# Residual rows loaded into the finished value columns of a weight tile, and the last two output blocks computed in column halves

## The chip, the cores and the metric

The kernel runs on one core of a Trainium2 chip. That core has five engines that run at the same time, each through its own list of instructions in order: TensorE for matrix products (PE in the profile, with its loads of the stationary operand listed apart as PEld), VectorE (DVE), ScalarE (ACT), GpSimd (POOL) and SyncE (SP). Data moves between the chip's main memory and the core's working memory (SBUF) by DMA. Here DMAs are started by SP, ACT and POOL, each with a queue of its own: q1 is SP's, q10 is ACT's and q0 is POOL's. Matrix products accumulate in PSUM, which has eight banks of 512 float32 columns per partition.

The metric is the device time of one execution in microseconds (us). Before the change it is 259.9 us, the median of three runs (259.37 to 260.32 us).

## The reference

The input `x` has 2048 tokens of width 512. It is normalised once. One branch is attention with 32 heads of width 16, in which a token sees itself and the 255 tokens before it. The other is a gated MLP whose gate mixes all tokens. The output is `x` plus both branches, so every block of output rows needs the same block of rows of `x` once more: these rows are called the residual here.

```python
def _A_ref(x, wqkv, wo):
    B, S, D = x.shape          # 1, 2048, 512
    H = 32; Dh = D // H; W = 256
    qkv = (lambda x, *d: x.transpose(*d))((x @ wqkv).reshape(B, S, 3, H, Dh), 2, 0, 3, 1, 4)
    q, k, v = (qkv[0], qkv[1], qkv[2])
    scores = jnp.einsum('bhqd,bhkd->bhqk', q, k) * Dh ** (-0.5)
    idx = jnp.arange(S)
    mask = (idx[:, None] - idx[None, :] >= 0) & (idx[:, None] - idx[None, :] < W)
    p = _softmax(jnp.where(mask[None, None], scores, -1000000000.0), axis=-1)
    o = jnp.einsum('bhqk,bhkd->bhqd', p, v)
    return (lambda x, *d: x.transpose(*d))(o, 0, 2, 1, 3).reshape(B, S, D) @ wo

def _B_ref(x, w_in, w_sp, b_sp, w_out):
    z = _gelu(jnp.einsum('bsd,df->bsf', x, w_in))       # 2048 x 1376
    z1 = z[..., :688]
    z2 = _layernorm(z[..., 688:], axis=-1)
    g = jnp.einsum('ts,bsf->btf', w_sp, z2) + b_sp[None, :, None]
    return jnp.einsum('bsf,fd->bsd', z1 * g, w_out)

xn = _layernorm(A_x, axis=-1)
return A_x + _A_ref(xn, A_wqkv, A_wo) + _B_ref(xn, B_w_in, B_w_sp, B_b_sp, B_w_out)
```

## The kernel before

Tokens are cut into 16 blocks of 128 rows (`n` = 0 to 15). Heads are cut into four groups of eight (`G` = 0 to 3). The order of all work is written out by hand in three strings, `STAGE1`, `STAGE2` and `STAGE3`: each token such as `O,15,k,0,1` names a step by a letter and gives its arguments. The table `ops` maps letters to functions, and `run` calls them in the order of the string. Each engine then works through its own share of the steps in that order, and waits only where its data or its buffer is not ready.

Stage 1 normalises `x`, computes the gated activations and starts the projections. Stage 2 runs the attention: for each group, `S` computes scores (L429, PE), `X` takes their exponentials (L443, ACT), `M` masks them (L452 and L460, DVE), `V` multiplies by the values (L510, PE), and `N` normalises the result and transposes it into `oT` (L518 to L531, DVE). Between these, PE does projections (`Q`, `K`, `P`: L339 and L394), the token mixing (`H`, L551) and at the end the output products. `F` and `G` spread projected queries and keys by DMAs on the POOL queue (L366 and L387; for the last head groups `F,3,3` and `G,3,3` are the last of them). `u` transposes a block of the MLP's result by a DMA on the SP queue (L564).

An output block `n` is made by these steps:

- `r,n` (`load_xres`, L574): POOL issues a DMA that loads the block's 128 x 512 residual rows into a tile `x_ch`. The tile comes from the pool `cpool`, which gives it two buffers. The load of one block therefore waits until the add of the block two loads earlier has read its buffer.
- `O,n,bank,c0,c1` (`out_u`, L580): PE multiplies by the MLP's output weights, six products of 128 x 512 in all; `R,n,bank,c0,c1` (`out_o`, L586) adds the attention's output product, four more, one for each head group, into the same PSUM bank.
- `o,n,bank` (`keep_out`, L594): DVE adds PSUM and the residual into a tile `out_sb`, also with two buffers.
- `v,n` (`store_out`, L601): a DMA writes 128 KB to the output. It is issued on POOL's queue for block 0 and on SP's for the others.

Banks `w` and `v` serve the blocks up to 11 in turn. In stage 3 the four banks that the scores used are free, and blocks 13, 12, 15 and 14 use the banks `i`, `j`, `k` and `l`. The adds come in the order 0 1 3 2 5 4 6 7 8 9 11 10 13 12 15 14.

The weights of all three projections stay in one tile, `wqkv`, of 128 partitions x 4 chunks x 1536 columns. Columns 0 to 1023 of each chunk are read by `Q` and `K`, columns 1024 to 1535 by `P` alone, whose last step stands early in stage 2.

Of the kernel before, what the change touches and what calls it, by code (L numbers as in the profile page):

```python
# [22 lines left out]
NDC = D // P  # L23
NG = 4
# [4 lines left out]
NFC = UPAD // P  # L29
# [113 lines left out]
H,13,1,v,6,7 K,3,2,w,2,4 H,13,1,v,7,13 k,3,2,w,D M,13 S,2,9,0 G,3,2 H,13,1,v,13,16 X,2,9,0  # L143
H,14,0,w,0,6 h,13,1,v M,14 u,8 V,22 M,15 r,1 S,3,0,0 H,14,0,w,6,7 Q,3,2,v,0,1 X,3,0,0 N,21,0
H,14,0,w,7,8 Q,3,2,v,1,2 H,14,0,w,8,10 Q,3,2,v,2,3 H,14,0,w,10,16 u,9 h,14,0,w S,3,0,1 V,23
X,3,0,1 N,21,1 H,14,1,w,0,3 N,22,0 Q,3,2,v,3,4 H,14,1,w,3,8 q,3,2,v,D S,3,1,0 H,14,1,w,8,16
X,3,1,0 M,0 F,3,2 u,10 M,1 H,15,0,v,0,7 h,14,1,w N,22,1 S,3,1,1 V,24 X,3,1,1 H,15,0,v,7,16 u,11
M,2 S,3,2,0 H,15,1,w,0,6 X,3,2,0 h,15,0,v Q,3,3,v,0,4 H,15,1,w,6,8 q,3,3,v,D u,12 S,3,2,1
H,15,1,w,8,9 M,3 F,3,3 K,3,3,v,0,2 X,3,2,1 H,15,1,w,9,13 N,23,0 K,3,3,v,2,3 H,15,1,w,13,15
K,3,3,v,3,4 N,23,1 H,15,1,w,15,16 k,3,3,v,A S,3,3,0 V,25 h,15,1,w X,3,3,0 N,24,0 O,1,v,0,1  # L150
O,0,w,0,6 N,24,1 S,3,3,1 M,4 R,0,w,0,1 X,3,3,1 O,1,v,1,2 R,0,w,1,2 O,1,v,2,4 R,0,w,2,3 O,1,v,4,6
R,0,w,3,4 R,1,v,0,1 o,0,w S,3,4,0 R,1,v,1,4 X,3,4,0 M,5 v,0 O,3,w,0,3 o,1,v V,26 v,1 r,3 N,25,0
r,2 S,3,4,1 O,2,v,0,2 X,3,4,1 O,3,w,3,6 M,6 R,3,w,0,2 N,25,1 O,2,v,2,3 R,3,w,2,3 O,2,v,3,4 M,7
S,3,5,0 O,2,v,4,6 X,3,5,0 R,3,w,3,4 R,2,v,0,4 o,3,w v,3 r,5 V,27 o,2,v S,3,5,1 N,26,0 v,2 r,4
O,5,w,0,5 u,13 X,3,5,1 G,3,3 O,4,v,0,1 O,5,w,5,6 R,5,w,0,2 O,4,v,1,2 M,8 S,3,6,0 O,4,v,2,6
X,3,6,0 N,26,1 R,4,v,0,2 M,9 R,5,w,2,4 R,4,v,2,4 o,5,w S,3,6,1 o,4,v V,28 r,7 X,3,6,1 v,4 r,6
N,27,0 O,6,w,0,1 O,7,v,0,1 v,5 O,6,w,1,3 O,7,v,1,3 O,6,w,3,4 M,10 S,3,7,0 O,7,v,3,5 N,27,1
X,3,7,0 O,6,w,4,6 R,6,w,0,2 O,7,v,5,6 R,6,w,2,4 R,7,v,0,1 o,6,w S,3,7,1 R,7,v,1,3 X,3,7,1 v,6
r,8 O,8,w,0,1 u,14 R,7,v,3,4 O,8,w,1,6 o,7,v M,11 r,9 v,7 O,9,v,0,1 S,3,8,0 M,12 V,29 X,3,8,0
N,28,0 O,9,v,1,3 R,8,w,0,1 O,9,v,3,5 N,28,1 R,8,w,1,3 S,3,8,1 O,9,v,5,6 X,3,8,1 R,8,w,3,4  # L160
R,9,v,0,4 o,8,w r,10 O,11,w,0,6 o,9,v M,13 v,9 r,11 v,8 O,10,v,0,1 M,14 S,3,9,0 u,15 V,30
X,3,9,0
"""

STAGE3 = """
N,29,0 R,11,w,0,1 O,10,v,1,2 R,11,w,1,2 O,10,v,2,5 N,29,1 R,11,w,2,3 O,13,i,0,1 O,10,v,5,6 M,15
# [9 lines left out]
def kernel(  # L176
# [31 lines left out]
    oT = pers.tile([P, NG, S_TOK], BF, name="oT")  # L208
# [14 lines left out]
    banks = {"v": w0[:], "w": w1[:]}  # L223
# [345 lines left out]
    x_tiles = {}  # L569
    out_tiles = {}  # L570

    def load_xres(n):
        x_ch = cpool.tile([P, D], BF, name="x_ch")
        nc.gpsimd.dma_start(out=x_ch[:], in_=x2[n * P : (n + 1) * P, :])  # L574
# [16 lines left out]
    def keep_out(n, bank):  # L591
        out_sb = cpool.tile([P, D], BF, name="out_sb")
        out_tiles[n] = out_sb
        nc.vector.tensor_tensor(  # L594
            out=out_sb[:], in0=banks[bank], in1=x_tiles.pop(n)[:], op=ALU.add
        )

    def store_out(n):

        eng = nc.gpsimd if n == 0 else nc.sync  # L600
        eng.dma_start(out=out2[n * P : (n + 1) * P, :], in_=out_tiles.pop(n)[:])  # L601

    def set_o():
# [80 lines left out]
    for r0 in (0, 64):  # L684
        nc.gpsimd.affine_select(
            out=mask[r0 : r0 + 64, 0, :], in_=mask[r0 : r0 + 64, 0, :], pattern=[[-1, 64]],
# [3 lines left out]
            out=mask[r0 : r0 + 64, 1, :], in_=mask[r0 : r0 + 64, 1, :], pattern=[[1, 64]],  # L690
# [54 lines left out]
```

## Time and profile before

| what | value |
|---|---|
| median of three runs | 259.9 us |
| the profiled execution, its own time | 258.91 us |
| its span, from its first to its last instruction | 257.1 us |
| VectorE, ScalarE, GpSimd busy | 186.0, 181.0, 90.9 us |
| residual loads, 16 on POOL's queue, 128 KB each | 3.8 us from issue to landing (median) |
| output stores, 15 on SP's queue, 128 KB each | 1.9 us from issue to landing (median) |
| the output store on POOL's queue | 2.1 us |

A row of the timeline gives the start and the length of a group of alike instructions on one engine, in us from the start of the span. Then come the engine, the line of the program, the operation, the tile written and the tile read with their shapes, and the count. In brackets stands how long the engine was idle before it, and what ended that idle time. The ends of matmuls are modelled by the profiler, and since matmuls are pipelined, the distance between the starts of two neighbours is shorter than the length of one. Some matmul records can be missing. "DMA to landing" is the time from the issue of a DMA to the arrival of its last byte. A row of the view by form gives a group's total busy time and the mean length of one instruction in nanoseconds.

### The profile page before, as it was taken

To read this page: it belongs to the slowest core of one execution; us is meant where nothing else is said; L and a number is where in the kernel's file an instruction comes from. 1 tells how busy PE (TensorE), PEld (TensorE's weight loads), DVE (VectorE), ACT (ScalarE), POOL (GpSimd) and SP (SyncE) were. 2 spreads that over 40 slices of the span, in tenths; PEclk is the share of its full clock that TensorE was granted. 3 is DMA by queue.
4 is the path that set the end of the run, shared out by engine and by line. 5 is a ranking of instruction groups with operands and counts; after the bars stand their busy time and mean duration, and the time that the engine had idled before them with its cause. 6 is when DMAs were issued, how large, how long until landed. Compare 5 with 4: busy or idle time off the path is not lost. (4 is left out here: it accounts for less than half of the span.)

```text
span 257.1 us, 9010 instructions
## 1 busy us (share of the span) xinstructions
PE 248.5 (97%) x3880; PEld 137.1 (53%) x3916; DVE 186.0 (72%) x410; ACT 181.0 (70%) x142; POOL 90.9 (35%) x170
## 2 busy tenths in 40 slices
PE   7999999999999999999999999999999999999994
PEld 6565555433456555555555655655656544444541
DVE  4887877888797686778684776857877577667763
ACT  3686476899978687777868777776777786767400
POOL 7524110430015176017197055505545142511120
PEclk9999999999999999999999999999999999999999
DMA  7995743289404897749669476997755532764433
GB/s 237 362 247 98 118 82 83 61 134 234 96 3 95 102 145 144 129 98 170 116 122 165 105 101 118 123 161 128 156 123 96 94 74 84 112 128 116 115 102 102
DMA packets 69847, 32.65 MB, mean 127 GB/s; under 512 B 60800, under 2 KB 66912, under 8 KB 69808
## 3 DMA queue, kind: packets, MB, share of 16 engines
q1 hardware_dynamic: 64288, 21.19, 44.9%
q0 software_dynamic: 4576, 9.71, 17.6%
q10 hardware_dynamic: 944, 1.19, 1.3%
q8 instruction: 30, 0.49, 0.9%
q14 instruction: 9, 0.07, 0.1%
HBM read 8.41 MB, written 2.10 MB: 41 GB/s over the span
## 5 line engine op out<-in xcount | busy, mean ns | idle before, releaser
L443 ACT ACTIVATE E<-sS 128x2048 bf16<-128x2048 f32 x76 | 142.6, 1877 | 41.9 <-PE sS L429 40.8
L551 PE MATMUL w<-z,wspT 128*128 128x344 bf16 x512 | 92.6, 310 | 0.7 <-DVE z1u L558 0.2
L551 PEld LDWEIGHTS <-wspT 128*128 128x128 bf16 x512 | 46.9, 98 | 31.5 <-issue 5.9
L387 POOL DMA_DIRECT2D kbd<-kz x48 | 29.5, 622 | 59.8 <-DVE kz L379 57.7
L366 POOL DMA_DIRECT2D q<-qs x54 | 28.0, 527 | 30.5 <-DVE qs L355 23.1
L452 DVE TENSOR_TENSOR E<-E,mask 128x1024 bf16<-128x1024 bf16 x52 | 34.7, 676 | 4.3 <-ACT E L443 4.3
L339 PE MATMUL w<-xnT,wqkv 128*128 128x512 bf16 x106 | 35.7, 380 | 0.7 <-issue 0.3
L429 PE MATMUL sS<-q,kbd 32*128 32x320 bf16 (+4 forms) x816 | 30.4, 244 | 0.5 <-ACT E L443 0.2
L558 DVE SCALAR_TENSOR_TENSOR z1u<-w,b_all,z1u 128x344 bf16<-128x344 f32 x32 | 18.2, 568 | 16.3 <-PE w L551 16.2
L518 DVE STREAM_TRANSPOSE a<-oP 128x512 f32<-128x512 f32 x32 | 22.7, 709 | 4.7 <-PE oP L510 4.6
L309 PEld LDWEIGHTS <-xnT 128*128 128x128 bf16 x208 | 18.3, 98 | 12.4
L510 PE MATMUL oP<-E,v_all 64*17 64x256 bf16 (+3 forms) x1920 | 24.7, 230 | 0.0
L510 PEld LDWEIGHTS <-v_all 64*17 64x17 bf16 x1920 | 20.2, 85 | 8.4 <-issue 8.1
L429 PEld LDWEIGHTS <-kbd 32*128 32x128 bf16 x816 | 12.3, 92 | 22.3 <-issue 19.9
L580 PE MATMUL w<-w_out_sb,z1u 128*128 128x512 bf16 x67 | 19.1, 380 | 0.7 <-issue 0.3
L574 POOL DMA_DIRECT2D x_ch<-in_A_x_dram x16 | 8.8, 552 | 27.8 <-DVE out_sb L594 23.5
L339 PEld LDWEIGHTS <-wqkv 128*128 128x128 bf16 x128 | 12.1, 98 | 9.7 <-issue 1.2
L327 DVE BATCH_NORM_STATS2 st<-z 128x6 f32<-128x344 bf16 x32 | 14.4, 493 | 2.7 <-ACT z L322 2.7
L394 PE MATMUL w<-wqkv,xnT 128*128 128x512 bf16 x63 | 16.2, 379 | 0.0
L531 DVE STREAM_TRANSPOSE oT<-b 128x256 bf16<-128x256 bf16 x32 | 14.3, 445 | 1.1
L379 DVE CAST kz<-w 128x256 bf16<-128x256 f32 x26 | 9.8, 418 | 6.8 <-PE w L339 5.3
L580 PEld LDWEIGHTS <-z1u 128*128 128x128 bf16 x96 | 8.6, 97 | 10.2 <-issue 1.2
(90 smaller groups left out, 248.4 us busy)
## 6 DMA issues: line engine op xcount, KB each, us to landing
kbd<-kz POOLq DMA_DIRECT2D x48, 64.0 KB, 3.4
q<-qs POOLq DMA_DIRECT2D x36, 64.0 KB, 3.1
x_ch<-in_A_x_dram POOLq DMA_DIRECT2D x16, 128.0 KB, 3.8
out_dram<-out_sb SPq DMA_DIRECT2D x15, 128.0 KB, 1.9
wqkv<-in_A_wqkv_dram SPq DMA_DIRECT2D x1, 1536.0 KB, 12.0
xs<-in_A_x_dram SPq DMA_DIRECT2D x2, 512.0 KB, 7.2
kbd<-kz SPq DMA_DIRECT2D x16, 64.0 KB, 2.2
q<-qs SPq DMA_DIRECT2D x14, 64.0 KB, 2.0
```

Source lines behind the costliest of these rows:

```text
L309: nc.tensor.matmul(zp[:, lo:hi], lhsT=xcT[:, n, c, :] if n < NCEN else xnT[:, c, n * P : (n + 1) * P], rhs=w_in_sb[:, c, f0 + lo : f0 + hi ...
L339: nc.tensor.matmul(banks[bank], lhsT=wqkv[:, c, col : col + P], rhs=xnT[:, c, tok : tok + 512], start=(c == 0), stop=(c == NDC - 1),)
L366: eng.dma_start(out=q2[h : P : 2, e, c : c + w], in_=t[64 * e : 64 * e + 64, src0 + at : src0 + at + w],)
L387: eng.dma_start(out=kbd[h : P : 2, slot : slot + 4, e, :], in_=t[64 * e : 64 * e + 64, h, :].rearrange("p (k m) -> p k m", k=4),)
L429: nc.tensor.matmul(s_bank(s)[:, off + o : off + o + w], lhsT=kbd[32 * s : 32 * s + 32, slot, ee, :], rhs=q2[32 * s : 32 * s + 32, ee, c : ...
L443: nc.scalar.activation(out=dst, in_=src, func=ACT.Exp, scale=SM_SCALE)
L452: nc.vector.tensor_tensor(out=reg, in0=reg, in1=mask[:].rearrange("p a m -> p (a m)").unsqueeze(1).to_broadcast([P, 8, 128]), op=ALU.mult,)
L510: nc.tensor.matmul(skip_group_check=True, **args)
L518: nc.vector.transpose(out=a32[:].rearrange("p e c r -> p (e c r)"), in_=oP[i % 2][:])
L551: nc.tensor.matmul(banks[bank][:, 0:FQ], lhsT=w[:, c, :], rhs=z2[:, c, half * FQ : (half + 1) * FQ], start=(c == 0), stop=(c == NB - 1),)
L558: nc.vector.scalar_tensor_tensor(out=u, in0=banks[bank][:, 0:FQ], scalar=b_all[:, n : n + 1], in1=u, op0=ALU.add, op1=ALU.mult,)
L580: nc.tensor.matmul(banks[bank], lhsT=uT[:, c, :], rhs=w_out_sb[:, c, :], start=(c == 0), stop=False)
```

## The change

Three things change.

1. A residual load no longer writes a tile of its own. `load_xres(n)` writes into `wqkv[:, n % 4, 1024:1536]`, so there are four places in turn. The loads `r,2` to `r,15` stand earlier in the written order: `r,2` and `r,3` among the scores of the last head group, and each later one right behind the add that frees its place. The pool `cpool` gets four buffers instead of two, for `out_sb` alone.
2. The stores of blocks 1 and 2 go on POOL's queue, as that of block 0 did.
3. Blocks 15 and 14 are computed in two column halves of 256, each half in a PSUM bank of its own (`k` and `w`, `l` and `v`). Twenty products of 512 columns become forty of 256. Each half has its own add, and its own store of 64 KB: the left halves on SP's queue, the right halves on ACT's.

```diff
-X,3,0,1 N,21,1 H,14,1,w,0,3 N,22,0 Q,3,2,v,3,4 H,14,1,w,3,8 q,3,2,v,D S,3,1,0 H,14,1,w,8,16
+X,3,0,1 N,21,1 H,14,1,w,0,3 N,22,0 Q,3,2,v,3,4 H,14,1,w,3,8 q,3,2,v,D S,3,1,0 r,2 H,14,1,w,8,16
 X,3,1,0 M,0 F,3,2 u,10 M,1 H,15,0,v,0,7 h,14,1,w N,22,1 S,3,1,1 V,24 X,3,1,1 H,15,0,v,7,16 u,11
-M,2 S,3,2,0 H,15,1,w,0,6 X,3,2,0 h,15,0,v Q,3,3,v,0,4 H,15,1,w,6,8 q,3,3,v,D u,12 S,3,2,1
+M,2 S,3,2,0 r,3 H,15,1,w,0,6 X,3,2,0 h,15,0,v Q,3,3,v,0,4 H,15,1,w,6,8 q,3,3,v,D u,12 S,3,2,1
 H,15,1,w,8,9 M,3 F,3,3 K,3,3,v,0,2 X,3,2,1 H,15,1,w,9,13 N,23,0 K,3,3,v,2,3 H,15,1,w,13,15
 K,3,3,v,3,4 N,23,1 H,15,1,w,15,16 k,3,3,v,A S,3,3,0 V,25 h,15,1,w X,3,3,0 N,24,0 O,1,v,0,1
 O,0,w,0,6 N,24,1 S,3,3,1 M,4 R,0,w,0,1 X,3,3,1 O,1,v,1,2 R,0,w,1,2 O,1,v,2,4 R,0,w,2,3 O,1,v,4,6
-R,0,w,3,4 R,1,v,0,1 o,0,w S,3,4,0 R,1,v,1,4 X,3,4,0 M,5 v,0 O,3,w,0,3 o,1,v V,26 v,1 r,3 N,25,0
-r,2 S,3,4,1 O,2,v,0,2 X,3,4,1 O,3,w,3,6 M,6 R,3,w,0,2 N,25,1 O,2,v,2,3 R,3,w,2,3 O,2,v,3,4 M,7
-S,3,5,0 O,2,v,4,6 X,3,5,0 R,3,w,3,4 R,2,v,0,4 o,3,w v,3 r,5 V,27 o,2,v S,3,5,1 N,26,0 v,2 r,4
-O,5,w,0,5 u,13 X,3,5,1 G,3,3 O,4,v,0,1 O,5,w,5,6 R,5,w,0,2 O,4,v,1,2 M,8 S,3,6,0 O,4,v,2,6
-X,3,6,0 N,26,1 R,4,v,0,2 M,9 R,5,w,2,4 R,4,v,2,4 o,5,w S,3,6,1 o,4,v V,28 r,7 X,3,6,1 v,4 r,6
+R,0,w,3,4 R,1,v,0,1 o,0,w r,4 S,3,4,0 R,1,v,1,4 X,3,4,0 M,5 v,0 O,3,w,0,3 o,1,v r,5 V,26 v,1
+N,25,0 S,3,4,1 O,2,v,0,2 X,3,4,1 O,3,w,3,6 M,6 R,3,w,0,2 N,25,1 O,2,v,2,3 R,3,w,2,3 O,2,v,3,4
+M,7 S,3,5,0 O,2,v,4,6 X,3,5,0 R,3,w,3,4 R,2,v,0,4 o,3,w r,7 v,3 V,27 o,2,v r,6 S,3,5,1 N,26,0
+v,2 O,5,w,0,5 u,13 X,3,5,1 G,3,3 O,4,v,0,1 O,5,w,5,6 R,5,w,0,2 O,4,v,1,2 M,8 S,3,6,0 O,4,v,2,6
+X,3,6,0 N,26,1 R,4,v,0,2 M,9 R,5,w,2,4 R,4,v,2,4 o,5,w r,9 S,3,6,1 o,4,v r,8 V,28 X,3,6,1 v,4
 N,27,0 O,6,w,0,1 O,7,v,0,1 v,5 O,6,w,1,3 O,7,v,1,3 O,6,w,3,4 M,10 S,3,7,0 O,7,v,3,5 N,27,1
-X,3,7,0 O,6,w,4,6 R,6,w,0,2 O,7,v,5,6 R,6,w,2,4 R,7,v,0,1 o,6,w S,3,7,1 R,7,v,1,3 X,3,7,1 v,6
-r,8 O,8,w,0,1 u,14 R,7,v,3,4 O,8,w,1,6 o,7,v M,11 r,9 v,7 O,9,v,0,1 S,3,8,0 M,12 V,29 X,3,8,0
+X,3,7,0 O,6,w,4,6 R,6,w,0,2 O,7,v,5,6 R,6,w,2,4 R,7,v,0,1 o,6,w r,10 S,3,7,1 R,7,v,1,3 X,3,7,1
+v,6 O,8,w,0,1 u,14 R,7,v,3,4 O,8,w,1,6 o,7,v r,11 M,11 v,7 O,9,v,0,1 S,3,8,0 M,12 V,29 X,3,8,0
 N,28,0 O,9,v,1,3 R,8,w,0,1 O,9,v,3,5 N,28,1 R,8,w,1,3 S,3,8,1 O,9,v,5,6 X,3,8,1 R,8,w,3,4
-R,9,v,0,4 o,8,w r,10 O,11,w,0,6 o,9,v M,13 v,9 r,11 v,8 O,10,v,0,1 M,14 S,3,9,0 u,15 V,30
+R,9,v,0,4 o,8,w r,12 O,11,w,0,6 o,9,v r,13 M,13 v,9 v,8 O,10,v,0,1 M,14 S,3,9,0 u,15 V,30
 X,3,9,0
...
-O,13,i,1,3 R,11,w,3,4 R,10,v,0,1 O,12,j,0,1 o,11,w V,31 v,11 r,13 N,30,0 O,13,i,3,5 R,10,v,1,2
-O,15,k,0,1 R,10,v,2,4 O,13,i,5,6 o,10,v O,15,k,1,2 O,12,j,1,2 R,13,i,0,1 N,30,1 O,12,j,2,6 v,10
-r,12 R,13,i,1,3 R,12,j,0,1 R,13,i,3,4 V,32 o,13,i N,31,0 O,15,k,2,3 v,13 r,15 R,12,j,1,2
-O,14,l,0,1 R,12,j,2,4 O,15,k,3,4 o,12,j O,14,l,1,5 N,31,1 v,12 r,14 O,15,k,4,5 O,14,l,5,6
-O,15,k,5,6 R,15,k,0,4 R,14,l,0,4 o,15,k v,15 o,14,l v,14
+O,13,i,1,3 R,11,w,3,4 R,10,v,0,1 O,12,j,0,1 o,11,w r,15 V,31 v,11 N,30,0 O,13,i,3,5 R,10,v,1,2
+f,15,0,k,0,1 f,15,1,w,0,1 R,10,v,2,4 O,13,i,5,6 o,10,v r,14 f,15,0,k,1,2 f,15,1,w,1,2 O,12,j,1,2
+R,13,i,0,1 N,30,1 O,12,j,2,6 v,10 R,13,i,1,3 R,12,j,0,1 R,13,i,3,4 V,32 o,13,i N,31,0
+f,15,0,k,2,3 f,15,1,w,2,3 v,13 R,12,j,1,2 f,14,0,l,0,1 f,14,1,v,0,1 R,12,j,2,4 f,15,0,k,3,4
+f,15,1,w,3,4 o,12,j f,14,0,l,1,5 f,14,1,v,1,5 N,31,1 v,12 f,15,0,k,4,5 f,15,1,w,4,5 f,14,0,l,5,6
+f,14,1,v,5,6 f,15,0,k,5,6 f,15,1,w,5,6 g,15,0,k,0,4 g,15,1,w,0,4 g,14,0,l,0,4 g,14,1,v,0,4
+x,15,0,k x,15,1,w x,14,0,l x,14,1,v
...
     def load_xres(n):
-        x_ch = cpool.tile([P, D], BF, name="x_ch")
-        nc.gpsimd.dma_start(out=x_ch[:], in_=x2[n * P : (n + 1) * P, :])
+
+        x_ch = wqkv[:, n % NDC, 2 * D : 3 * D]
+        nc.gpsimd.dma_start(out=x_ch, in_=x2[n * P : (n + 1) * P, :])
         x_tiles[n] = x_ch
...
+    def out_u_half(n, half, bank, c0, c1):
+        uT = z1u[:, n, :].rearrange("p (c t) -> p c t", c=NFC)
+        for c in range(c0, c1):
+            nc.tensor.matmul(
+                banks[bank][:, 0:256], lhsT=uT[:, c, :],
+                rhs=w_out_sb[:, c, 256 * half : 256 * half + 256],
+                start=(c == 0), stop=False,
+            )
+
+    def out_o_half(n, half, bank, c0, c1):
+        for G in range(c0, c1):
+            nc.tensor.matmul(
+                banks[bank][:, 0:256], lhsT=oT[:, G, n * P : (n + 1) * P],
+                rhs=wo_sb[:, G, 256 * half : 256 * half + 256],
+                start=False, stop=(G == NG - 1),
+            )
+
+    def store_half(n, half, bank):
+        if half == 0:
+            out_tiles[n] = cpool.tile([P, D], BF, name="out_sb")
+        c = slice(256 * half, 256 * half + 256)
+        nc.vector.tensor_tensor(
+            out=out_tiles[n][:, c], in0=banks[bank][:, 0:256], in1=x_tiles[n][:, c], op=ALU.add
+        )
+        eng = nc.scalar if half else nc.sync
+        eng.dma_start(out=out2[n * P : (n + 1) * P, c], in_=out_tiles[n][:, c])
 
     def store_out(n):
 
-        eng = nc.gpsimd if n == 0 else nc.sync
+        eng = nc.gpsimd if n < 3 else nc.sync
         eng.dma_start(out=out2[n * P : (n + 1) * P, :], in_=out_tiles.pop(n)[:])
...
-        "w": load_wsp, "r": load_xres, "m": set_o,
+        "w": load_wsp, "f": out_u_half, "g": out_o_half, "x": store_half, "r": load_xres, "m": set_o,
...
-    cpool = ctx.enter_context(tc.tile_pool(name="cpool", bufs=2))
+    cpool = ctx.enter_context(tc.tile_pool(name="cpool", bufs=4))
```

More of the change, by code (lines that the diff above doesn't have):

```diff
@@ L594, in keep_out @@
         nc.vector.tensor_tensor(
-            out=out_sb[:], in0=banks[bank], in1=x_tiles.pop(n)[:], op=ALU.add
+            out=out_sb[:], in0=banks[bank], in1=x_tiles.pop(n), op=ALU.add
         )
+    def out_u_half(n, half, bank, c0, c1):
[22 more added lines that the diff above has]
+        eng.dma_start(out=out2[n * P : (n + 1) * P, c], in_=out_tiles[n][:, c])
     def store_out(n):
-        eng = nc.gpsimd if n == 0 else nc.sync
+        eng = nc.gpsimd if n < 3 else nc.sync
         eng.dma_start(out=out2[n * P : (n + 1) * P, :], in_=out_tiles.pop(n)[:])
```

## The prediction

> **What bounds the kernel now.** I read the page's busy times first, then the timeline of the last 30 us, then what ends the profile after the last add.
>
> ```profile
> span 257.1 us, 9010 instructions
> PE 248.5 (97%) x3880; PEld 137.1 (53%) x3916; DVE 186.0 (72%) x410; ACT 181.0 (70%) x142; POOL 90.9 (35%) x170
> ```
>
> TensorE is busy in 97% of the span, so only two kinds of places can give time: where TensorE stands still, and what comes after its last product. The tail, in the timeline:
>
> ```profile
> 251.30 0.45 DVE L531 STREAM_TRANSPOSE oT<-b 128x256 bf16<-128x256 bf16 x1
> 251.55 1.61 PEld L586 LDWEIGHTS <-oT 128*128 128x128 bf16 x8
> 251.77 1.03 PE L586 MATMUL tk<-wo_sb,oT 128*128 128x512 bf16 x4
> 252.63 1.03 PE L586 MATMUL tl<-wo_sb,oT 128*128 128x512 bf16 x4
> 252.83 0.69 DVE L594 TENSOR_TENSOR out_sb<-tk,x_ch 128x512 bf16<-128x512 f32 x1 [1.08 <-PE tk L586]
> 253.74 0.69 DVE L594 TENSOR_TENSOR out_sb<-tl,x_ch 128x512 bf16<-128x512 f32 x1 [0.21 <-PE tl L586]
> 254.46 0.33 SPq L601 DMA_DIRECT2D out_dram<-out_sb  x1
> ```
>
> The last product ends at 252.63 + 1.03 = 253.66, the last add runs from 253.74 to 254.43, and its store is issued at 254.46. The page's chain of waits puts something else at this place, the last residual load:
>
> ```profile
> 246.79 0.54 POOL x_ch L574
> ...
> 251.23 2.43 DMA x_ch<-in_A_x_dram
> ...
> 253.74 0.69 DVE out_sb L594
> ```
>
> The load ends at 251.23 + 2.43 = 253.66, in the same hundredth as the product. So the chain's name for the end is half a coincidence: without the load the product would hold the add just as long. What follows is in the views of the store's line and of the program's last line:
>
> ```profile
> L601 SPq DMA_DIRECT2D out_dram<-out_sb x3: 332/333/333, 251.0 to 254.5; - x3
> ...
> DMA to landing us min/median/max: 1.7/1.7/1.7
> ```
>
> ```profile
> L740 SPq DRAIN  x3: 7/7/7, 256.2 to 256.5; - x3
> ```
>
> The store lands at 254.46 + 1.7 = 256.16, and the closing of the program takes the remaining 0.94 us.
>
> The other place is where TensorE stands still. Looking through its rows from 200 us on, I find one real stall; the short gaps at each change of matmul shape recur throughout and stay.
>
> ```profile
> 229.78 0.81 PE L586 MATMUL w<-wo_sb,oT 128*128 128x512 bf16 x3
> ...
> 230.86 0.60 PE L586 MATMUL w<-wo_sb,oT 128*128 128x512 bf16 x2
> 230.91 0.69 DVE L594 TENSOR_TENSOR out_sb<-w,x_ch 128x512 bf16<-128x512 f32 x1 [1.67 <-DMA x_ch<-in_A_x_dram]
> 231.04 1.88 ACT L443 ACTIVATE E<-sS 128x2048 bf16<-128x2048 f32 x1 [0.78 <-PE sS L429]
> ...
> 231.65 0.38 PE L580 MATMUL w<-w_out_sb,z1u 128*128 128x512 bf16 x1 [0.19 <-DVE out_sb L594]
> ...
> 233.47 0.40 PE L429 MATMUL sS<-q,kbd 32*128 32x64 bf16 x12
> ```
>
> ```profile
> L574 POOL DMA_DIRECT2D x_ch<-in_A_x_dram x2: 563/565/567, 226.0 to 226.6; - x2
> ...
> DMA to landing us min/median/max: 4.0/4.1/4.3
> ```
>
> The residual of block 6 is issued at 226.6 and lands 4.3 us later, at 230.9. The add `o,6` waits for it, and `O,8` on PE waits for the bank `w` that the add empties.
>
> **The change part by part.**
>
> *Residual loads moved earlier.* The pitch of 512-column products is (1.03 - 0.38) / 3 = 0.216 us in the rows of `tk` and `tl`. After the pair at 230.86 the next would start at 231.29; it starts at 231.65. The stall is 0.36 us. With the change `r,6` is issued behind `o,2`, where `r,4` is issued now (220.50, below), so ten microseconds before its add. What is late next? The second product of the group at 229.78 is the last of block 6: it starts at 230.00 and ends 0.38 later, the add could run from 230.42 to 231.11, and 231.29 is later. So PE no longer waits. The next scores at 233.47 would move to 233.11 and need the exponential that ends at 231.04 + 1.88 = 232.92. That wait leaves little:
>
> ```profile
> 212.94 1.88 ACT L443 ACTIVATE E<-sS 128x2048 bf16<-128x2048 f32 x1 [0.72 <-PE sS L429]
> ...
> 214.85 0.14 PEld L429 LDWEIGHTS <-kbd 32*128 32x128 bf16 x8
> ```
>
> Here scores followed an exponential's end (214.82) by 0.03, so 0.19 is enough. All later work follows PE. I take **-0.36 us**, with bounds 0 and -0.36. At the end `r,14` is issued behind `o,10`, where `r,12` goes now (246.79 in the chain, against 251.23), so the last add waits for its product alone: `tk`'s add starts 0.03 behind its product, `tl`'s 0.08, **-0.05 us**.
>
> The moved loads share POOL's queue with the spreading DMAs. `r,2` and `r,3` fall into idle stretches of that queue, 3.15 us ahead of the spreads at 197.96 and the time after them:
>
> ```profile
> 197.96 2.08 POOL L366 DMA_DIRECT2D q<-qs  x4 [3.15 <-DVE qs L355]
> ...
> 203.44 1.03 PE L339 MATMUL w<-xnT,wqkv 128*128 128x512 bf16 x3
> ```
>
> For `r,4` to `r,6` the place that matters is ahead of `G,3,3`:
>
> ```profile
> 220.50 0.55 POOL L574 DMA_DIRECT2D x_ch<-in_A_x_dram  x1 [0.32 <-DVE out_sb L594]
> ...
> 221.04 2.47 POOL L387 DMA_DIRECT2D kbd<-kz  x4
> ...
> 227.93 0.40 PE L429 MATMUL sS<-q,kbd 32*128 32x64 bf16 x12
> ```
>
> ```profile
> L387 POOL DMA_DIRECT2D kbd<-kz x2: 615/616/617, 222.3 to 222.9; - x2
> ...
> DMA to landing us min/median/max: 4.8/4.8/4.8
> ```
>
> One DMA stands between `o,2` and `G,3,3` now, two after (`r,6` and the store `v,2`, both behind the same add): `G,3,3` starts 0.55 us later. Its last DMA lands at 222.9 + 4.8 = 227.7. The scores at 227.93 need the first and third, for one half of the heads; the other half comes one exponential later. The third, issued 0.6 earlier, should land at about 227.1 and then at 227.7, still in time. I cost it at nothing; if its landing is as late as the fourth's, the scores start at 228.25, +0.32 us. SP's queue loses `v,1` and `v,2`, and `u,13` behind them is issued up to 0.9 us sooner; its result serves a block of stage 3. Nothing for that, nor for the four `out_sb` buffers, since no add waits for a store in the rows.
>
> *Forty products of 256 for twenty of 512.* Each half has its own weight load. The trace has no 128-row product of 256 columns; the nearest are the gate's pairs of 512 and 176, each with its own load (a timeline row names the first form of its group):
>
> ```profile
> 44.85 1.33 PE L309 MATMUL zb<-w_in_sb,xnT 128*128 128x512 bf16 x8
> 46.01 1.33 PE L309 MATMUL zo<-w_in_sb,xnT 128*128 128x512 bf16 x8
> 47.18 1.03 PE L339 MATMUL w<-xnT,wqkv 128*128 128x512 bf16 x4
> ```
>
> ```profile
> L586 PEld LDWEIGHTS <-oT 128*128 128x128 bf16 x40 | 3.7, 98 | 4.8 <-issue 0.7 <-DVE oT L531 0.3
> ```
>
> From 44.85 to 47.18 there are eight pairs: 0.291 us each, so 0.075 for 176 columns. A weight load is listed with 98 ns and hides even there. On the line from (176, 0.075) to (512, 0.216), 256 columns take 0.109, two 0.218 instead of 0.216: 20 x 0.002 = **+0.04 us**. The lower bound is 0. The upper, each load of 0.098 standing bare ahead of 0.109: 40 x 0.098 = +3.9 us. I take the line's value, as the 176-column product lies on the same side.
>
> The Trainium skill ("TensorE: Matmul & The Clock Gate", Back-to-back issue gap) speaks against the halves: in streams of weight load and product it gives about 81 ns at 128 columns, against 56 without the loads. By that surplus of 25 ns the sum would be 1.0 us more, an estimate; the 0.075 us at 176 columns stands against it.
>
> *The add of a half.* The nearest DVE row that reads 128 x 256 float32 from PSUM is a cast:
>
> ```profile
> L379 DVE CAST kz<-w 128x256 bf16<-128x256 f32 x26 | 9.8, 418 | 6.8 <-PE w L339 5.3
> ```
>
> So 0.42 for 0.69: **-0.27 us** at the end, since PE makes four products of a half in 0.44 and DVE keeps up. The last product starts 0.11 us later than that of 512 columns would and is as much shorter.
>
> *The half stores.* ACT has nothing to do in the last two of the page's 40 slices:
>
> ```profile
> ACT  3686476899978687777868777776777786767400
> ```
>
> So its queue is free, and the two queues never issue at once, as the adds lie 0.44 apart and an issue takes 0.33. The last store carries 64 KB in place of 128.
>
> ```profile
> q<-qs SPq DMA_DIRECT2D x14, 64.0 KB, 2.0
> ...
> xs<-in_A_x_dram ACTq DMA_DIRECT2D x1, 128.0 KB, 2.8
> ```
>
> Rows of half the size (2.0) are no faster than the last store's 1.7. Bounds: 0.85 us sooner, if all of the 1.7 went with the bytes, and 1.1 later, by ACT's one small load. I take 0, as the nearest rows have equal time at unequal size. The Trainium skill ("DMA: Bandwidth & Descriptors", Anatomy of one DMA, SWDGE path) splits a DMA into a fixed 2.0 us and bytes over 436 GB/s; an estimate by it is 0.15 us sooner, which would make the sum -0.79.
>
> **The sum:** -0.36 - 0.05 + 0.04 - 0.27 = -0.64 us, a span of 256.46. The profiled execution took 258.91 us, 1.81 more than its span and 0.99 less than the median of the runs; taking the shift to the median, 259.9 - 0.64 = 259.26, forecast **259.3 us**.
>
> **The rivals.**
>
> *The stall moves instead of going.* `G,3,3`'s third DMA lands late (+0.32), or the scores after 233 us wait for the exponential, and the 0.36 is given back: about 259.6 us. For it speaks that the next exponential ends only 0.19 us before the scores would start.
>
> *The smaller store lands sooner*, anywhere up to 0.85 us: 258.4 to 259.1, middle 258.8. For it: store landings differ by what else moves, and nothing does at the end. Against: equal times at 64 and 128 KB.
>
> *Weight loads come out from under the 256-column products* (slower). Place: the last 40 products, behind one another on PE. Price: 40 times the bare part; from 16 ns each it eats the 0.64 us, and wholly bare it gives 259.9 - 0.64 + 3.9 = 263.1 us. Against it stands the pair's 0.291 us. The skill's surplus of 25 ns, weighed above, is one point of this case: 260.3 us, which counts as no change here.
>
> *The loads into `wqkv` are taken for writes to the whole tile* (the change doesn't do what it says). Then `Q,3,3`, due at 203.44, waits for `r,3`. `r,3` would go out behind the spreads, at 197.96 + 2.08 = 200.04, and land 4.0 to 4.3 later like the loads at 226, at 204.0 to 204.3: a stall of 0.6 to 0.9 us, and as much again if the loads wait behind earlier projections, up to 261 us. Against it: the weight loads from `oT` at 251.55 start while a transpose into another part of `oT` ends at 251.75, so waits go by parts of a tile.
>
> **How the numbers follow.** Forecast 0.48 (258.9 to 259.6 with the scatter of a median of three), the moved stall 0.22, the sooner store 0.17, bare weight loads 0.06, whole-tile waits 0.07. The measurement tells some 0.3%, or 0.78 us, from no change. My forecast lies just inside that. Faster than 259.12: 0.4 of the forecast (0.19), all of the sooner store, 0.04 of the moved stall: 0.40. Slower than 260.68: bare loads, most of the whole-tile waits and a little scatter, 0.14. No change 0.46. The range takes in the store's lower bound (258.4) and reaches up over the moved stall to 260.4.
>
> **What would show it.** Right: the add of block 6 waits for PE, not for a DMA; PE runs from 230.9 on without the wait for `out_sb`; the forty products have a pitch of 0.109; the last add takes 0.42; the last store is issued 0.3 us behind the last product's end plus that add. Wrong: a pitch over 0.12, a weight load of `kbd` or `wqkv` that waits for a DMA, a store on ACT's queue that takes over 2 us, or a POOL queue that ends after the stores.

## The result and the profile after

The changed kernel takes 258.65 us (median of 22 runs, 257.89 to 260.97) against 259.89 us (22 runs, 258.41 to 261.22) for the kernel before on the same chip. The ratio is 0.9953 with a 95% interval of 0.9938 to 0.9968: 1.22 us faster, between 0.83 and 1.61. The forecast was 0.64 us faster. The direction and the range held. The forecast size is about half of what was measured.

The page of the changed kernel:

```profile
span 256.9 us, 9051 instructions
PE 248.8 (97%) x3900; PEld 139.3 (54%) x3936; DVE 186.2 (72%) x412; ACT 181.0 (70%) x142; POOL 92.0 (36%) x172
PE 93%; ACT 3%; issue 1%; DMA 1%; DVE 1%
```

The profiled execution took 258.61 us. Its span is only 0.2 us under the 257.1 of before, much less than the medians differ by. The paragraph on reading two spans, below, shows why. The chain of waits no longer names the residual loads.

The timeline around the old stall, in the changed kernel (start, duration, engine, line, operation; in brackets the idle time before it and what ended it):

```profile
225.85 0.40 PE L431 MATMUL sS<-q,kbd 32*128 32x128 bf16 x16
...
228.49 0.40 PE L431 MATMUL sS<-q,kbd 32*128 32x64 bf16 x12
...
230.97 0.69 DVE L597 TENSOR_TENSOR out_sb<-w,wqkv 128x512 bf16<-128x512 f32 x1 [1.19 <-PE w L589]
231.08 0.40 PE L431 MATMUL sS<-q,kbd 32*128 32x64 bf16 x12
231.41 0.60 PE L589 MATMUL w<-wo_sb,oT 128*128 128x512 bf16 x2
231.85 0.38 PE L583 MATMUL w<-w_out_sb,z1u 128*128 128x512 bf16 x1
...
233.68 0.40 PE L431 MATMUL sS<-q,kbd 32*128 32x64 bf16 x12
```

The add of block 6 at 230.97 now waits for its product, not for a DMA, and runs well before `w` is needed again. The next product into `w` starts at 231.85, which is 231.41 plus two pitches of 0.216. Nothing is lost. The scores that were 233.47 - 230.53 = 2.94 us apart in the kernel before are 233.68 - 231.08 = 2.60 apart: 0.34 us is gone from this place.

The tail:

```profile
252.01 0.60 PE L613 MATMUL tk<-wo_sb,oT 128*128 128x256 bf16 x4
252.44 0.60 PE L613 MATMUL w<-wo_sb,oT 128*128 128x256 bf16 x4
252.88 0.60 PE L613 MATMUL tl<-wo_sb,oT 128*128 128x256 bf16 x4
...
253.32 0.60 PE L613 MATMUL w<-wo_sb,oT 128*128 128x256 bf16 x4
253.52 0.42 DVE L623 TENSOR_TENSOR out_sb<-tl,wqkv 128x256 bf16<-128x256 f32 x1
...
253.96 0.42 DVE L623 TENSOR_TENSOR out_sb<-w,wqkv 128x256 bf16<-128x256 f32 x1
```

Twelve products of 256 columns, each with its own weight load, lie between 252.01 and 253.32: a pitch of 0.109 us. The last product ends at 253.92, the last add follows 0.04 later and takes 0.42. Then come the stores of the halves, and the closing of the program:

```profile
L627 SPq DMA_DIRECT2D out_dram<-out_sb x2: 332/332/332, 253.1 to 254.0; - x2
L627 ACTq DMA_DIRECT2D out_dram<-out_sb x2: 362/364/366, 253.5 to 254.4; - x2
...
DMA to landing us min/median/max: 1.5/1.5/1.6
```

```profile
L771 SPq DRAIN  x3: 7/7/7, 256.1 to 256.4; - x3
```

The 64 KB stores land in 1.5 to 1.6 us, where the 128 KB store of before took 1.7.

**Reading two spans against each other.** The last scores with sixteen products ahead of the stall start at 225.29 in the profile of before and at 225.85 in this one. The scores that start at 194.65 before start at 195.21 here: the same 0.56 us, ahead of the first moved load. So this execution came late to the stretch that the change touches. In the fourteen profiles of this study the scores at 225.29 start anywhere from 225.23 to 226.81, and the unchanged kernel alone spans 225.29 to 226.81. Nor does any difference arise in between: from the scores at 194.65 to those at 225.29 pass 30.64 us in all five profiles of these two kernels. I therefore measure every profile from the scores at 225.29 on, in three pieces: to the scores behind block 6's add (233.47 in the profile of before), from there to the end of the last add, and from there to the end of the span. The first two together are called the stretch. The values are taken from the trace, where times and spans stand with more digits than in the views:

| kernel | scores start | to the scores behind block 6's add | from there to the end of the last add | from there to the end |
|---|---|---|---|---|
| before | 225.29 | 8.18 | 20.96 | 2.63 |
| before, second profile | 225.43 | 8.25 | 20.95 | 2.62 |
| before, third profile | 226.81 | 8.33 | 20.92 | 2.65 |
| whole change | 225.85 | 7.83 | 20.70 | 2.52 |
| whole change, second profile | 226.21 | 7.83 | 20.70 | 2.53 |

Read this way one profile of each gives -0.61 us in the stretch (28.53 for 29.14) and -0.11 us behind it.

### The profile page after: what moved, and what is told of

Read it like the earlier page. It is cut to its first block, busy times and chain, and to the rows that moved or that the text cites. A ratio compares the mean times of both kernels' runs of the same rounds, so it can differ in the third digit from the quotient of the medians.

```text
span 256.9 us, 9051 instructions
## 1 busy us (share of the span) xinstructions
PE 248.8 (97%) x3900; PEld 139.3 (54%) x3936; DVE 186.2 (72%) x412; ACT 181.0 (70%) x142; POOL 92.0 (36%) x172
## 4 chain that ended last, share of the span: by engine, by line
PE 93%; ACT 3%; issue 1%; DMA 1%; DVE 1%
PE w L553 31%; PE sS L431 10%; PE w L341 10%; PE oP L512 8%; PE w L583 6%; PE zb L311 5%; PE za L311 5%; PE zo L311 5%; PE w L396 4%; PE w L589 4%; ACT E L445 2%; DMA xs<-in_A_x_dram 1%; PE w L286 1%; PE w L605 1%; PE tj L583 1%
## 5 line engine op out<-in xcount | busy, mean ns | idle before, releaser
L577 POOL DMA_DIRECT2D wqkv<-in_A_x_dram x16 | 8.9, 558 | 28.3 <-DVE out_sb L597 27.5
L589 PE MATMUL w<-wo_sb,oT 128*128 128x512 bf16 x47 | 13.8, 380 | 0.0
```

What stands on the lines that cost most here:

```text
L589: nc.tensor.matmul(banks[bank], lhsT=oT[:, G, n * P : (n + 1) * P], rhs=wo_sb[:, G, :], start=False, stop=(G == NG - 1),)
```

## The experiments

Ratios are to the kernel before in the same set of runs, with 95% intervals. The kernel before has medians of 259.58, 259.70 and 259.77 us in the three sets. The stall at block 6 is worked out as above: the start of the next `w_out` product into `w`, less the start of the pair of `wo` products ahead of it and two pitches (0.43).

**The kernel before, unchanged.** No edit.

> The kernel before, unchanged. The theory of one stall says: the ratio to the kernel before is 1.000 within its interval, and in the profile the add of block 6 waits for its residual and PE loses about 0.36 us behind it, as in the first profile. The rival of varying waits says: this profile shows other or longer waits for residual loads than the first one (0.5 us of PE time or more in sum, or another block), because loads that are issued just in time land by chance sooner or later.

Measured: 259.65 us, ratio 1.0012 (0.9994 to 1.0031). This is what two measurements of one kernel can differ by. Its profile has a stall of 231.87 - 231.00 - 0.43 = 0.44 us.

**Residuals alone.** The early loads into `wqkv`, four `out_sb` buffers, the last two blocks whole, and the stores of blocks 1 and 2 back on SP's queue (part of the edit shown).

```diff
-f,15,0,k,5,6 f,15,1,w,5,6 g,15,0,k,0,4 g,15,1,w,0,4 g,14,0,l,0,4 g,14,1,v,0,4
-x,15,0,k x,15,1,w x,14,0,l x,14,1,v
+O,15,k,5,6 R,15,k,0,4 R,14,l,0,4 o,15,k v,15 o,14,l v,14
```

> The four places in the weight tile and the earlier loads alone; the last two blocks in one piece, stores of blocks 1 and 2 on SP's queue. The theory of one stall says 0.36 + 0.05 = 0.41 us less than before, ratio 0.9984. The rival of varying waits says 0.8 us or more less, ratio 0.997 or lower. The rival that the tail carries the gain says no difference, ratio above 0.999.

> The residual part alone once more, beside the whole change. The halves are then worth the difference to the whole change: 0.27 us of the add, and 0.2 us of the last store (landing 1.5 us in the profile after, 1.7 before), 0.45 us or 0.17% in sum if nothing else differs; 0.25 us if the store's landing does not count.

Measured, in two sets: 258.86 us, 0.9982 (0.9967 to 0.9996), and 259.24 us, 0.9981 (0.9966 to 0.9996). That is -0.47 and -0.49 us. In both profiles the stretch is 28.75 us against 29.14 to 29.25, so 0.39 to 0.50 shorter, and what follows takes 2.64, as before. The first piece is 7.83, as in the whole change; the second is 20.92, where the kernel before has 20.92 to 20.96. So 0.35 to 0.50 belongs to block 6 and at most 0.04 to the last add, for the predicted 0.36 and 0.05.

**Halves alone.** The kernel before with the column halves and the two queues; the residuals load into two `x_ch` buffers at their old places.

```diff
-O,15,k,5,6 R,15,k,0,4 R,14,l,0,4 o,15,k v,15 o,14,l v,14
+f,15,0,k,5,6 f,15,1,w,5,6 g,15,0,k,0,4 g,15,1,w,0,4 g,14,0,l,0,4 g,14,1,v,0,4
+x,15,0,k x,15,1,w x,14,0,l x,14,1,v
```

> The column halves of the last two blocks and their two queues alone; residual loads in two buffers and in the old order. The last add's residual still lands at about 253.7 us in the profile, so the halves save the half add: 0.25 us less than before, ratio 0.9990, by the theory of one stall and by that of varying waits. The rival that the tail carries the gain says 0.7 us or more less, ratio 0.9973 or lower.

Measured: 259.75 us, ratio 1.0008 (0.9983 to 1.0033). No gain is measured, where the terms of the halves promised 0.23 us; the interval alone would not exclude that much. The profile does: from the scores behind block 6's add to the end of the last add pass 20.95 us, as before. The tail of its timeline shows why:

```profile
252.90 0.55 POOL L577 DMA_DIRECT2D x_ch<-in_A_x_dram  x1 [1.30 <-DVE out_sb L597]
...
254.22 0.42 DVE L623 TENSOR_TENSOR out_sb<-tk,x_ch 128x256 bf16<-128x256 f32 x1 [0.80 <-DMA x_ch<-in_A_x_dram]
...
254.34 0.60 PE L613 MATMUL tl<-wo_sb,oT 128*128 128x256 bf16 x4
...
255.33 0.42 DVE L623 TENSOR_TENSOR out_sb<-tl,x_ch 128x256 bf16<-128x256 f32 x1 [0.36 <-PE tl L613]
255.67 0.41 DVE L623 TENSOR_TENSOR out_sb<-w,x_ch 128x256 bf16<-128x256 f32 x1
```

The first half of block 14 is ready at 254.34 + 0.60 = 254.94, but its add starts at 255.33. The row names PE, which had long been done. The other input, the residual issued at 252.90, is what is left, and 255.33 is 2.4 us behind its issue, the time that this load took at this place in the kernel before. So the half stood ready and waited for a transfer, and two half adds (0.34 + 0.41 = 0.75 us) now follow the landing, where one whole add of 0.69 did. The halves are worth something only when the residual is there early. Behind the last add this kernel takes 2.90 us to close, 0.27 more than before; the run with the stores back on SP's queue, below, shows the cause.

The same profile holds the longest stall at block 6 of the study:

```profile
231.60 0.60 PE L589 MATMUL w<-wo_sb,oT 128*128 128x512 bf16 x2
...
232.57 0.69 DVE L597 TENSOR_TENSOR out_sb<-w,x_ch 128x512 bf16<-128x512 f32 x1 [2.60 <-DMA x_ch<-in_A_x_dram]
233.31 0.38 PE L583 MATMUL w<-w_out_sb,z1u 128*128 128x512 bf16 x1 [1.11 <-DVE out_sb L597]
```

PE loses 233.31 - 231.60 - 0.43 = 1.28 us, at a place that the halves do not touch. That is why the first piece takes 9.10 us here.

**Whole change with the loads at their old places.** The loads still go into the four columns of `wqkv`, and all else is as in the whole change, but each `r` is written where it stood in the kernel before (two of the places shown).

```diff
-... M,2 S,3,2,0 r,3 H,15,1,w,0,6 ...
+... M,2 S,3,2,0 H,15,1,w,0,6 ...
-... o,4,v r,8 V,28 X,3,6,1 v,4
+... o,4,v V,28 r,7 X,3,6,1 v,4 r,6
```

> The whole change, but the residual loads stand where they stood before in the written order. If four places are what counts, POOL issues block 6's load behind the last key spread at about 224 us, it lands by 228.5, ahead of its add, and the time is that of the whole change, ratio 0.9953 or 0.997 within the interval. If the written order is what counts, the add of block 6 waits again and the time lies 0.36 us above that of the whole change.

Measured: 258.62 us, ratio 0.9962 (0.9944 to 0.9980), the same as the whole change. Its stretch is 28.53 us. At block 6 the load is not what the add waits for. The timeline:

```profile
224.92 1.13 POOL L577 DMA_DIRECT2D wqkv<-in_A_x_dram  x2
...
225.84 1.29 DVE L597 TENSOR_TENSOR out_sb<-w,wqkv 128x512 bf16<-128x512 f32 x2 [0.63 <-PE w L589]
...
231.29 0.69 DVE L597 TENSOR_TENSOR out_sb<-w,wqkv 128x512 bf16<-128x512 f32 x1 [1.18 <-PE w L589]
```

With four places POOL need not wait for the adds of blocks 5 and 4 (the pair at 225.84) to free two of them, as it must with two: `r,7` and `r,6` are issued from 224.92 on, ahead of both adds, land 2.3 and 2.6 us later, and block 6's add at 231.29 waits for its product alone. With the four `out_sb` buffers of the whole change, it is the number of places that counts here, not where the loads are written.

**Only block 6's residual moved.** The kernel before, except that `r,6` goes into `wqkv` and is issued right behind `r,4`, some five and a half microseconds earlier. All else, the two `out_sb` buffers too, is as it was.

```diff
-... S,3,5,1 N,26,0 v,2 r,4
+... S,3,5,1 N,26,0 v,2 r,4 r,6
-        x_ch = cpool.tile([P, D], BF, name="x_ch")
+        x_ch = wqkv[:, 2, 2 * D : 3 * D] if n == 6 else cpool.tile([P, D], BF, name="x_ch")[:]
```

> The kernel before with one edit: block 6's residual alone goes to a place in the weight tile, issued ahead of the last key spread. If the wait for block 6's load is all that the residual part of the change took away before the tail, and if it varies from run to run as the profiles so far show (0.36, 0.44 and 1.28 us of PE time), the ratio is about 0.9975 (0.6 us less), near that of the residual part alone (0.9982). If a stall of 0.36 us is all there is, 0.9986. If other waits for residuals matter too, 0.9995 or above.

Measured: 259.59 us, ratio 0.9997 (0.9977 to 1.0018). No gain is measured, though the one load that ended the stall was taken away; the interval does not exclude 0.36 us. In the profile the first piece is 8.14 us, 0.03 to 0.19 less than before. The timeline:

```profile
232.29 0.60 PE L586 MATMUL w<-wo_sb,oT 128*128 128x512 bf16 x2
232.30 0.69 DVE L594 TENSOR_TENSOR out_sb<-w,wqkv 128x512 bf16<-128x512 f32 x1 [1.64 <-DMA out_dram<-out_sb]
...
233.05 0.38 PE L580 MATMUL w<-w_out_sb,z1u 128*128 128x512 bf16 x1 [0.15 <-DVE out_sb L594]
```

and the part of the chain of waits that leads to the add (start, duration, what):

```profile
227.71 4.46 DMA out_dram<-out_sb
...
232.30 0.70 DVE out_sb L594
```

The add of block 6 still starts late, now because the buffer that it writes is held by an earlier store, 4.46 us on its way. The stall is 233.05 - 232.29 - 0.43 = 0.33 us, nearly as long as the 0.36 with the residual in the first profile. A second wait stood behind the first at this add, and the profile names only the one that ends last.

**Two `out_sb` buffers under the whole change.**

```diff
-    cpool = ctx.enter_context(tc.tile_pool(name="cpool", bufs=4))
+    cpool = ctx.enter_context(tc.tile_pool(name="cpool", bufs=2))
```

> The whole change with two output buffers instead of four. If the wait that showed in the run with block 6's load alone (its add waits for the store of block 5) is the second half of what the change removed, the add of block 6 waits for a store here too, PE loses 0.3 to 0.5 us behind it, and the time lies that much above the whole change's: ratio to before about 0.997 against 0.9953. If the buffers are worth nothing, as the prediction had it, the ratio is that of the whole change.

Measured: 258.75 us, ratio 0.9971 (0.9953 to 0.9989), beside 0.9960 for the whole change in the same set. The intervals do not tell 0.29 us apart. The profile does: its stretch is 28.86 us, 0.33 longer than with four buffers, and one wait has come that the four buffers do not have:

```profile
226.46 0.69 DVE L597 TENSOR_TENSOR out_sb<-w,wqkv 128x512 bf16<-128x512 f32 x1 [0.47 <-DMA out_dram<-out_sb]
226.65 0.39 PE L583 MATMUL w<-w_out_sb,z1u 128*128 128x512 bf16 x1
227.20 1.02 PE L583 MATMUL w<-w_out_sb,z1u 128*128 128x512 bf16 x3 [0.17 <-DVE out_sb L597]
```

After 226.65 the next product was due one pitch later, at 226.87; it starts at 227.20, 0.33 us late. The wait is for a store and costs PE a third of a microsecond, as expected, but it falls on an add one pair of blocks earlier: there the store of block 2, put on POOL's queue by the change and 5.0 us on its way, holds the buffer. At block 6 the add waits for its product alone. So this run doesn't show what the buffers are worth without that store on POOL's queue.

**One queue for the half stores.**

```diff
-        eng = nc.scalar if half else nc.sync
+        eng = nc.sync
```

> The whole change with all four half stores on SP's queue. The adds lie 0.44 us apart and an issue takes 0.33, so by the prediction the second queue brings nothing: the same ratio as the whole change, 0.9953 to 0.997. If the second queue is worth something, each half store on the one queue is issued later than its add allows, and the time is 0.2 us or more above.

Measured: 258.70 us, ratio 0.9967 (0.9949 to 0.9986); stretch 28.53, and 2.60 us behind it against 2.52 and 2.53. The last store is issued 0.09 us behind the last add in place of 0.03. So the second queue is worth less than 0.1 us in the profile, and nothing that the times can tell.

**Stores of blocks 1 and 2 back on SP's queue.**

```diff
-        eng = nc.gpsimd if n < 3 else nc.sync
+        eng = nc.gpsimd if n == 0 else nc.sync
```

> The whole change with the stores of blocks 1 and 2 back on SP's queue, so nothing stands between block 6's load and the last key spread on POOL's queue. The prediction costs the two stores at nothing: the ratio of the whole change, 0.9953 to 0.997. If the later key spread costs something, 0.3 us less than the whole change.

Measured: 259.13 us, ratio 0.9977 (0.9961 to 0.9993). Its stretch is 28.53 us, as in the whole change; behind it the program takes 2.88 us to close instead of 2.52 to 2.53. The views of SP's waits and of the program's last line show the cause; the second row counts SP's checks of a signal (EVENT_SEMAPHORE) from 255.5 us to just ahead of the first DRAIN. First the whole change:

```profile
SPq L771 <- DMA out_dram<-out_sb: 1.2, 3, 0.4
L771 SPq EVENT_SEMAPHORE  x2: 28/28/28, 255.5 to 256.0; - x2
```

and with the two stores back on SP's queue:

```profile
SPq L771 <- DMA out_dram<-out_sb: 1.6, 2, 1.1
L771 SPq EVENT_SEMAPHORE  x7: 27/28/28, 255.5 to 255.9; - x7
L771 SPq DRAIN  x3: 7/7/7, 256.0 to 256.3; - x3
```

At the close SP checks one after another, some 0.06 us apart, that earlier DMAs have landed. In the whole change the last half store is the last that it asks for: that wait ends at 256.00, and the first DRAIN follows 0.07 later. Here the last two stores are asked for early in the row. The wait for the last one ends at 255.53, but six more checks, already fulfilled, follow it, and the DRAIN starts at 255.96, 0.43 later. The difference of 0.36 to 0.37 us is all of the longer close. The trace lists for each DMA of SP and ACT one of eight signals, used in turn: the halves bring two stores more and so shift the last ones to other signals, and taking two stores off SP's queue shifts them back. Halves alone, which also leaves these two stores on SP's queue, ends with the same seven checks. In the times it is seen less well: the median is 0.0010 to 0.0024 above the three others that hold the whole change or nearly so (0.9953, 0.9960, 0.9967), which fits 0.37 us (0.0014), but the intervals overlap.

**A third profile of the kernel before.** No edit.

> The kernel before once more, for one more profile. If block 6's wait varies from run to run, PE's loss behind it lies anywhere between 0.3 and 1.3 us; if the second profile's 0.44 and the first's 0.36 are typical and 1.28 was the halves' doing, it lies at 0.3 to 0.5.

Measured: 260.42 us, one run. The stall:

```profile
232.38 0.60 PE L586 MATMUL w<-wo_sb,oT 128*128 128x512 bf16 x2
...
233.32 0.38 PE L580 MATMUL w<-w_out_sb,z1u 128*128 128x512 bf16 x1 [0.34 <-DVE out_sb L594]
```

233.32 - 232.38 - 0.43 = 0.51 us. With the loads of before the stall has thus been 0.36, 0.44, 0.51 and 1.28 us in four executions, 0.65 on average; the longest is that of halves alone.

**The whole change again**, in one set with the parts. No edit.

> The whole change, unchanged, beside the other runs of this call: ratio 0.9953, and no wait of a block's add for a DMA in the profile.

Measured: 258.90 us, ratio 0.9960 (0.9944 to 0.9976), or -1.04 us. Against residuals alone in the same set (0.9981) the halves with early residuals are worth 0.0021, or 0.55 us, each ratio uncertain by 0.0015 or more. In the profiles they are worth 20.92 - 20.70 = 0.22 us up to the end of the last add and 0.11 behind it.

**Quarters for the last half block.** The last half of block 14 is made and added in two pieces of 128 columns, in the banks `v` and `i`, with one 64 KB store behind the second.

```diff
-... g,14,0,l,0,4 g,14,1,v,0,4
-x,15,0,k x,15,1,w x,14,0,l x,14,1,v
+... g,14,0,l,0,4 L,14,256,v L,14,384,i
+x,15,0,k x,15,1,w x,14,0,l s,14,256,v s,14,384,i
```

> The whole change with block 14's right half in two quarters of 128 columns, in banks of their own, and one store for both. The last add handles 128 columns: 0.13 us less by the line through 0.69 us at 512 and 0.42 us at 256. Twenty products of 128 columns for ten of 256 cost nothing if a weight load hides behind 128 columns too, so 0.13 us less than the whole change; if a load of 0.098 us sets the pace there, 20 x 0.098 - 10 x 0.109 = 0.87 us more in those places and 0.7 us slower than the whole change.

Measured: 258.11 us (7 runs, 257.96 to 258.90), ratio 0.9946 (0.9927 to 0.9966), the lowest of the study. It is faster than the kernel before. Against the whole change (0.9960 in the same set) the intervals overlap, and the profile does not bear out a gain:

```profile
252.72 0.39 PE L629 MATMUL w<-wo_sb,oT 128*128 128x128 bf16 x4
...
252.94 0.39 PE L629 MATMUL ti<-wo_sb,oT 128*128 128x128 bf16 x4
253.26 0.28 DVE L637 TENSOR_TENSOR out_sb<-w,wqkv 128x128 bf16<-128x128 f32 x1
253.46 0.28 DVE L637 TENSOR_TENSOR out_sb<-ti,wqkv 128x128 bf16<-128x128 f32 x1
```

The last product ends at 253.33, and its add begins only at 253.46: VectorE has two adds to follow one another in place of one, and is now what holds the end. From the scores (225.23) to the end of the last add (253.74) pass 28.50 us, 0.03 less than in the whole change, where 0.13 was expected.

## Why the prediction was right, and where its size was off

**The stall.** Predicted -0.36 us, with bounds 0 and -0.36. The mechanism was right: with the change the add waits for PE, and the scores come 0.34 us sooner. The size was taken from one execution, as if the stall were a constant. Four executions gave 0.36 to 1.28. The shown row was the shortest of them, so the bound of -0.36 was no bound. It is a race between PE and a load that took 4.0 to 4.8 us from issue to landing around there, and the price of a race is a distribution.

**"Nothing ... for the four `out_sb` buffers, since no add waits for a store in the rows."** This step failed as an argument, though its value held in the profile that it was read from. Rows of waits show the last wait only. The numbers to see how near the next one was stood in the profile of before:

```profile
L601 SPq DMA_DIRECT2D out_dram<-out_sb x2: 333/384/434, 226.3 to 226.7; - x2
...
DMA to landing us min/median/max: 3.9/3.9/3.9
```

The store that the add waited for with only block 6's residual moved is the first of such a pair. With 3.9 us it lands here at 230.2; the prediction has block 6's add ready to run at 230.42, and the residual lands half a microsecond behind that. So the store came 0.2 ahead of the add: it cost nothing in this execution, but by a narrow margin. By the same reckoning it came 0.1 to 0.2 ahead in the two other profiles of before, 0.3 behind with only block 6's residual moved (4.46 us), and 0.7 behind in halves alone (4.7 us). It is a second race. So the buffers were worth nothing in the plain profiles; they would have counted in the two executions where these DMAs took longest, and in one of them the profile shows it (0.33 us). The change has the early loads and the buffers together, and so none of this reached its sum. What the buffers are worth on average no run here isolates.

**The last add without its residual, -0.05.** Small either way: behind block 6, residuals alone take 20.92 us up to the end of the last add, where the three profiles of before take 20.92 to 20.96.

**Forty products of 256, +0.04.** Right to the last digit: a pitch of 0.109, as interpolated from 176 and 512 columns. The case of bare weight loads is out. The surplus of 25 ns per product that follows from the 81 and 56 ns of the Trainium skill at 128 columns ("TensorE: Matmul & The Clock Gate", Back-to-back issue gap) does not appear: by it, an estimate, the twelve products above would have taken 12 x 0.025 = 0.3 us more. At 128 columns themselves the kernel with quarters has a pitch of 0.055 us, not 0.081.

**The last add, -0.27.** Right in a kernel whose residuals are early (0.42 measured; -0.23 with the products' 0.04, and 20.92 - 20.70 = 0.22). The expectation for halves alone counted it as independent of the loads. Halves alone show that it isn't: without the early loads the piece that holds it is as long as before.

**The half store's landing, 0.** Off by 0.1: 1.5 to 1.6 us in place of 1.7. In five of the eight profiles with halves the end of the span follows the last add by 2.51 to 2.53 us, in place of 2.62 to 2.65 with a whole last store; with one queue for the half stores it follows by 2.60. In the other two, halves alone and the stores back on SP's queue, it follows by 2.90 and 2.88, though their stores land as fast: there the last checks come behind the last landing. The estimate by the Trainium skill that stood beside it ("DMA: Bandwidth & Descriptors", Anatomy of one DMA, SWDGE path), 0.15 sooner, was the better one, though its fixed part of 2.0 us alone is longer than the 1.5 to 1.7 measured; equal times of transfers of another kind at other places had weighed too much. Of the case "smaller store lands sooner" so much is true, though its middle of 0.43 is not.

**The stores of blocks 1 and 2, "Nothing for that".** This step failed too. With the halves they are worth 0.37 us at the close (2.88 for 2.52), through the order in which SP checks the landings. Without them the halves bring nothing: with the stores back on SP's queue the profile takes 28.53 + 2.88 = 31.41 us from the scores to the end, and residuals alone takes 28.75 + 2.64 = 31.39; the ratios (0.9977 and 0.9981) agree. That the change has both parts, so that the last store is again the last one checked, was luck: no row in the prediction speaks of it.

**POOL's order, 0.** Right. `G,3,3` goes out 225.85 - 222.13 = 3.72 us ahead of the scores in place of 225.29 - 221.04 = 4.25, so 0.53 later, for 0.55 predicted:

```profile
221.06 0.55 POOL L577 DMA_DIRECT2D wqkv<-in_A_x_dram  x1 [0.31 <-DVE out_sb L597]
221.59 0.54 POOL L632 DMA_DIRECT2D out_dram<-out_sb  x1
222.13 2.46 POOL L389 DMA_DIRECT2D kbd<-kz  x4
```

The scores that need it follow 2.64 us after the ones before them in both kernels. The stall did not move, neither to `G,3,3` nor to the exponential. Whole-tile waits cost nothing, but the place that the prediction named could not have shown them:

```profile
200.57 0.57 POOL L577 DMA_DIRECT2D wqkv<-in_A_x_dram  x1
...
204.00 1.03 PE L341 MATMUL w<-xnT,wqkv 128*128 128x512 bf16 x3
```

`r,3` landed 2.8 us after its issue, not 4.0 to 4.3, and so at 203.3, ahead of `Q,3,3`. Whether a wait for the whole tile is there and was fulfilled in time, the runs do not tell. From 225 us on the adds of the changed kernel wait for products alone, mostly in this row of the view of waits (us in total, times, longest):

```profile
DVE out_sb L597 <- PE w L589: 3.9, 7, 1.2
```

**The sum.** In the plain profiles the change is worth 0.35 to 0.50 us at block 6, 0.22 to 0.26 from there to the end of the last add, and 0.09 to 0.13 behind it: together -0.71 to -0.85 us, for -0.64 forecast. By the runs it is 1.22 us faster (0.83 to 1.61) and 1.04 (0.62 to 1.45). The direction and the places were thus right; that the sum came near is in part luck, since the buffers and the two stores on POOL's queue, both put at nothing, kept further losses away. That executions with a stall of the 1.28 us kind account for the rest, 0.2 to 0.5 us, is argued only: with the average of 0.65 for the stall the profiles would give about -1.0.

## What to carry to other kernels

A wait in a profile is the one that ended last; before you price its removal, work out when every other input and the output buffer of that instruction would have been free, from the rows of their own transfers. A wait that is a race with a DMA has no single price: take it from several executions. And parts of a change that meet at one instruction are not a sum: halves without early residuals, and one early residual without more buffers, each brought no gain that their runs could tell. The close of a program belongs to the sum too: here it depended on which store was checked last.

## What the runs showed of the hardware

- A weight load listed with 98 ns hides even behind products of 128 columns: in the kernel with quarters four products lie between 252.72 and 252.94, a pitch of 0.055 us, each with its own load.
- A 128 KB load of residual rows took 4.0 to 4.8 us around block 6, 2.3 to 2.6 us when issued a microsecond earlier (loads at their old places, from 224.92 on), and 2.4 us at the end of the program.
- SP closes the program with a row of checks that DMAs have landed, some 0.06 us apart, in a fixed order. A last store that was asked for early in the row cost 0.37 us (2.88 against 2.52 us behind the last add).
- Executions of one kernel drift apart before the stretch in question by up to 1.5 us (225.29 to 226.81 for the scores, before unchanged). Some of it is seen as a pause of PE that nothing in the profile ends, as in the third profile of before:

```profile
178.04 0.76 PE L510 MATMUL oP<-E,v_all 64*17 64x64 bf16 x55
179.25 0.27 PE L510 MATMUL oP<-E,v_all 64*17 64x128 bf16 x9 [0.45 <-issue]
```

Fifty-five of 64 products run, then PE waits 0.45 us for nothing that is recorded. Over a stretch of 30 us, from one and the same event to another, the profiles agree to 0.01 us for kernels with nothing left to race for (28.53 us in five profiles of the whole change and of its variants).
